# A Strassen form of the first channel product in a fused attention and MLP-mixer kernel

## Chip, cores and metric

The kernel runs on one core of one Trainium2 chip. The metric is the time of one execution on the device, in microseconds (us). A core has five engines that work side by side, each through its own queue in order: TensorE (PE; its weight loads are listed as PEld), VectorE (DVE), ScalarE (ACT), GpSimd (POOL) and SyncE (SP). TensorE writes its sums into eight banks of PSUM; the other engines empty them into SBUF.

## What is computed

Eight batches with eight heads of 576 rows and 64 columns; linear attention with random features (FAVOR), then a mixer of tokens and channels.

```python
q_s, k_s = q * scale, k * scale                  # scale = 64 ** -0.25
def phi(x):                                      # omega: 128 x 64
    h = x @ omega.T - sum(x * x) / 2
    return exp(h - max(h)) / sqrt(128)
kv, z = phi(k_s).T @ v, sum(phi(k_s), rows)
x = (phi(q_s) @ kv) / (phi(q_s) @ z + 1e-6)      # heads side by side: 8 x 576 x 512
h = relu(x.T @ w_tok1) @ w_tok2                  # 576 -> 256 -> 576, over tokens
u = x + h.T
out = u + relu(u @ w_ch1) @ w_ch2                # 512 -> 1536 -> 512, over channels
```

## The kernel before

The work is cut into *jobs*: one or a few instructions of one engine, with the jobs that they depend on and the places (PSUM banks, slots of rings of SBUF tiles) that they take and give back. The code makes all jobs in a fixed sequence, batch by batch, and numbers them as it goes. `ORDER` (L22) is a list, worked out beforehand, of these numbers: the order in which jobs are issued, and so the order of every engine's queue. Numbers below zero are warming matmuls. `SLOT` holds the place that each job takes; `MOVED` (L93) names the engine of a job where it is not the usual one. Nothing is planned while the kernel runs: each engine goes through its queue and waits on semaphores.

For each batch: `attention` (L521) projects keys and queries of four pairs of heads (L656, L668), takes exponentials on ScalarE (L514), the maximum over features on VectorE (L680) with a reciprocal (L682), scales v on GpSimd (`vs`, L689), multiplies keys with values (L701) and queries with that (L734, L736), and divides: `num_out` (L739) takes a reciprocal (L743) and a product (L744) on VectorE for each head, which gives `x`. `token_mix` (L764) makes the token products (L777, relu, L790), the sum `u` on VectorE (L793), and a DMA transposes `u` into `uT` (L798). Its first product needs all columns of `x` of its batch.

`channel_mix` (L955) works on 512 rows of a batch; the last 64 rows of all eight batches make a ninth chunk, the tail (`uTt`). Its first product is 12 blocks of 128 channels, each of four matmuls of 512 columns:

```python
for db in range(ND):
    nc.tensor.matmul(ps, wc1[:, db, cb * P : (cb + 1) * P], moving(db), start=(db == 0), stop=(db == ND - 1))
```

Each block takes a bank, and a relu (ScalarE, or VectorE by MOVED) writes it to `r3`. From batch 1 on the second product is done by `channel_out_fast` (L857) in a Strassen form (Winograd's): four sums `S` of quarters of `r3` on VectorE in two halves (L868 to L879), the sums `T` of weights made once (L448), seven products of 256 columns (L916), and seven `read`s on VectorE (L899) that add banks and `u` into the output tile `o`. Stores go out on SyncE's or ScalarE's queue, two of the tail on GpSimd's. Work of one batch's channel products, the next one's token products and the one after that's attention is interleaved in ORDER.

Of the kernel before, what the change touches and what calls it, by code (L numbers as in the profile page):

```python
# [9 lines left out]
FP32 = mybir.dt.float32  # L10
# [158 lines left out]
def kernel(  # L169
# [687 lines left out]
    def channel_out_fast(c, key, jr):  # L857
# [38 lines left out]
        def bank_of(b, j0):  # L896
            return (b, c, j0) if tail else (b, c)
# [173 lines left out]
```

## Time and profile before

| | |
|---|---|
| three runs | 276.75, 277.55, 277.63 us; median 277.55 |
| profiled execution | span 275.9 us, from the first to the last instruction; what lies around it is in the runs' times |
| busy share of the span | TensorE 97%, VectorE 81%, ScalarE 50%, GpSimd 33% |
| granted TensorE clock, mean | 0.996 |
| first product of the channels (L966) | 376 matmuls listed of batches 0 to 7, mean 379 ns each |
| second product (L916) | streams of 128x256 matmuls, mean 273 ns each |
| VectorE's largest groups | maximum L680 38.6 us, products L744 30.5, relus L292 27.7, reads L905 35.6 |
| start of the token products of batches 3 to 7 | 104.3, 133.5, 162.5, 189.5, 219.0 us |

A matmul's listed duration runs from its issue to the end of its passage through the array, and matmuls overlap; what one adds to a stream is the distance between two starts, which the chain of waits gives as time of a piece divided by its matmuls. Instructions of VectorE that are listed one behind the other can overlap a little in the same way.

### The profile page before, as it was taken

The numbers are of one execution on the slowest core, as the hardware profiler recorded it, in microseconds if no ns is written. First come the engines' busy times: TensorE is split into PE (matmuls) and PEld (weight loads), VectorE is DVE, ScalarE is ACT, GpSimd is POOL, SyncE is SP. The second block draws the span as 40 slices with busy tenths as digits, with TensorE's granted clock in tenths as the row PEclk, the third lists the DMA queues.
The fourth block names the chain that finished last, engine by engine and source line by source line (L and its number), as shares of the span: only waits on it lengthen the run. The fifth ranks groups of instructions, "written<-read, shape, count | busy, mean of one in ns | idle before, by whom it ended". The sixth has DMA issues, their size and how long they took to land.

```text
span 275.9 us, 6228 instructions
## 1 busy us (share of the span) xinstructions
PE 266.6 (97%) x2503; PEld 165.5 (60%) x2503; DVE 222.9 (81%) x462; ACT 138.1 (50%) x289; POOL 91.2 (33%) x115
## 2 busy tenths in 40 slices
PE   8789999999999999999999999999999999999993
PEld 3367455444567655755676656755676477446782
DVE  3897889876998799987999899978985992675992
ACT  3999941188685338734756456636654500040200
POOL 8994492063703490075019510600043000000001
PEclk9999999999999999999999999999999999999998
DMA  7999999999998999979989994840252304021125
GB/s 195 192 209 212 190 212 177 202 193 146 203 191 133 229 176 186 151 148 171 198 184 183 232 125 123 191 90 2 97 79 77 96 0 95 2 99 53 78 83 146
DMA packets 81292, 39.66 MB, mean 144 GB/s; under 512 B 63984, under 2 KB 77040, under 8 KB 81072
## 3 DMA queue, kind: packets, MB, share of 16 engines
q0 software_dynamic: 31744, 17.74, 44.2%
q1 hardware_dynamic: 47072, 15.50, 28.7%
q10 hardware_dynamic: 2448, 6.03, 5.6%
q8 instruction: 19, 0.31, 0.5%
q14 instruction: 9, 0.07, 0.1%
HBM read 35.95 MB, written 16.52 MB: 190 GB/s over the span
## 4 chain that ended last, share of the span: by engine, by line
PE 89%; DMA 6%; POOL 3%; DVE 0%; issue 0%; POOLq 0%
PE bank L966 33%; PE bank L916 25%; PE bank L777 5%; PE bank L790 5%; DMA w1m<-in_moe_w_tok_dram 4%; PE bank L1000 4%; PE bank L734 3%; PE bank L656 3%; PE bank L668 2%; PE bank L701 2%; DMA uT<-u 2%; POOL r L319 1%; PE bank L844 1%; PE bank L816 1%; PE bank L828 1%; PE bank L736 1%
## 5 line engine op out<-in xcount | busy, mean ns | idle before, releaser
L966 PE MATMUL bank<-uT,wc 128*128 128x512 f16 x376 | 90.4, 379 | 0.3 <-DMA uT<-u 0.3
L290 ACT ACTIVATE r<-bank 128x512 f16<-128x512 f32 (+1 forms) x84 | 46.9, 597 | 77.1 <-PE bank L966 62.0
L295 POOL TENSOR_TENSOR vs<-v,vs 128x512 f16<-128x512 f16 x31 | 33.2, 1074 | 91.2 <-DVE vs L682 60.5
L966 PEld LDWEIGHTS <-wc 128*128 128x128 f16 x424 | 38.3, 98 | 37.9 <-issue 1.1
L916 PEld LDWEIGHTS <-r 128*128 128x128 f16 x384 | 36.9, 98 | 8.1 <-issue 1.2
L514 ACT ACTIVATE kp<-bank 128x512 f16<-128x512 f32 x64 | 35.6, 622 | 10.4 <-PE bank L656 10.4
L514 ACT ACTIVATE qp<-bank 128x512 f16<-128x512 f32 x64 | 36.3, 616 | 8.9 <-PE bank L668 6.0
L680 DVE TENSOR_REDUCE km<-kp 128x8 f16<-128x1024 f16 x32 | 38.6, 1206 | 2.5 <-ACT kp L514 2.4
L292 DVE TENSOR_SCALAR r<-bank 128x512 f16<-128x512 f32 (+1 forms) x42 | 27.7, 672 | 12.0 <-PE bank L966 11.2
L744 DVE TENSOR_TENSOR x<-bank,rc 128x320 f16<-128x320 f32 x62 | 30.5, 492 | 2.1
L916 PEld LDWEIGHTS <-S 128*128 128x128 f16 x288 | 27.9, 98 | 5.4 <-issue 0.3
L905 DVE TENSOR_TENSOR o<-u,bank 128x512 f32<-128x512 f16 x28 | 19.0, 679 | 6.9 <-PE bank L916 6.8
L916 PE MATMUL bank<-T,r 128*128 128x256 f16 x192 | 23.8, 273 | 0.0
L916 PE MATMUL bank<-T,S 128*128 128x256 f16 x192 | 23.6, 273 | 0.0
L916 PE MATMUL bank<-wc,r 128*128 128x256 f16 x192 | 23.6, 273 | 0.0
L945 POOL DMA_DIRECT2D out_dram<-o x2 | 1.3, 648 | 60.9 <-issue 60.9
L793 DVE TENSOR_TENSOR u<-x,bank 128x512 f16<-128x512 f16 x28 | 17.8, 681 | 1.1 <-PE bank L790 1.0
L905 DVE TENSOR_TENSOR o<-o,bank 128x512 f32<-128x512 f32 (+1 forms) x27 | 16.6, 618 | 2.2 <-PE bank L916 1.6
L734 PEld LDWEIGHTS <-qp 128*128 128x128 f16 x256 | 13.8, 98 | 7.0 <-DVE kvsb L286 0.2
L734 PE MATMUL bank<-kvsb,qp 128*128 128x65 f16 x256 | 15.6, 193 | 0.0
L743 DVE RECIPROCAL rc<-bank 128x5 f32<-128x5 f32 x62 | 11.5, 186 | 4.1 <-PE bank L736 2.7
L701 PEld LDWEIGHTS <-kp 128*128 128x128 f16 x256 | 11.5, 98 | 5.1
(120 smaller groups left out, 376.3 us busy)
## 6 DMA issues: line engine op xcount, KB each, us to landing
out_dram<-o ACTq DMA_DIRECT2D x9, 512.0 KB, 2.6
q<-in_q_dram POOLq DMA_DIRECT2D x6, 576.0 KB, 7.2
wc<-in_moe_w_ch_dram POOLq DMA_DIRECT2D x4, 768.0 KB, 10.6
k<-in_k_dram POOLq DMA_DIRECT2D x6, 512.0 KB, 6.9
v<-in_v_dram POOLq DMA_DIRECT2D x6, 512.0 KB, 8.9
out_dram<-o SPq DMA_DIRECT2D x5, 512.0 KB, 3.9
r<-in_q_dram POOLq DMA_DIRECT2D x4, 288.0 KB, 7.3
v<-in_v_dram POOLq DMA_DIRECT2D x4, 256.0 KB, 8.7
```

The source lines that it names most:

```text
L290: nc.scalar.activation(out=out, in_=in_, func=AF.Relu)
L292: nc.vector.tensor_relu(out=out, in_=in_)
L295: (nc.gpsimd if eng == "POOL" else nc.vector).tensor_tensor(**kw)
L514: nc.scalar.activation(out=out, in_=in_, func=AF.Exp, bias=0.0, scale=1.0)
L680: nc.vector.reduce_max(out=mx, in_=kpv, axis=AX.X)
L701: nc.tensor.matmul(ps[:, i, :], kpv[:, 2 * i + j // 2, j % 2, :], vs[:, i * NJ + j, 0 : D + 1], start=(i == 0 and j == 0), stop=False, ski ...
L734: nc.tensor.matmul(ps[:, k, j * 65 : (j + 1) * 65], st, s[:, i, 0 : D + 1], start=True, stop=True)
L744: nc.vector.tensor_tensor(out=t_x[place("x", b)][:, :, (2 * hp + hs[0]) * D : (2 * hp + hs[0] + n) * D].rearrange("p j (i d) -> p i j d", ...
L793: nc.vector.tensor_tensor(out=t_u[place("u", b)][:, j, :], in0=t_x[place("x", b)][:, j, :], in1=bank(n), op=ALU.add)
L905: nc.vector.tensor_tensor(out=o, in0=a, in1=ps, op=ALU.add)
L916: nc.tensor.matmul(ps[:, j * DH : (j + 1) * DH], a[:, cb, j * P : (j + 1) * P], w[:, cb, :], start=(bank_of(b, j0) not in held and j == j0 ...
L966: nc.tensor.matmul(ps, wc1[:, db, cb * P : (cb + 1) * P], moving(db), start=(db == 0), stop=(db == ND - 1))
```

## The change

For batches 3 to 7 and the tail chunk (`FAST_IN = 3`) the first channel product is done by the new function `channel_in_fast`, in the same Strassen form. `u` and the weights are cut into quarters; four sums of quarters of `uT` (128x512 each) are made for each chunk (`usum` below), eight sums of weights (128x768 each) once, by `weight_sums`. The 1536 channels go in three thirds `m`. In each third there are seven products of four matmuls of 256 columns, in three banks: X takes P1, P6, P7 and P4 one after another, Y takes P2, Z takes P5 and P3. Between the products in X, ScalarE copies the bank to SBUF in fp32 (`keep`, three for each third). VectorE adds a kept product and a bank into `r3` (`join`, three for each third). Then come three relus: one from bank X (128x512), one over two quarters that stand in `r3` already (128x1024), one over the quarter from the third join (128x512).

The lists ORDER, SLOT and MOVED are new. For TensorE the new ORDER has the old sequence up to the last attention products of batch 3; from there on all engines have another order. MOVED now gives to GpSimd 16 of the 64 sums S, 11 of the 24 sums of `uT` and 3 of the 8 sums of weights, and gives to ScalarE 16 scalings `x = num * rc` (five activations each), of which batch 0 had two before. In ORDER the sums of GpSimd and VectorE's sums with two SBUF operands stand in turns.

Smaller edits: what were one job of a maximum with its reciprocal, or of a reciprocal with its product, are now two or three jobs with the same instructions (`km`, `kt_max`, `num_out`), with rings for their small tiles; the first and second halves' sums S depend on the sums that they read and no longer on the one before; the tail's output uses slots of `x` in place of `o`; the ring of `r1` has two places in place of three; five of the tail's stores change between SyncE's and ScalarE's queue. `SPLIT` and `HALVES` are empty, so what hangs on them is not issued.

```diff
+    FAST_IN = 3
+    SPLIT = ()
+    HALVES = ()
...
+    t_sum = sb([P, 2, DC // 2], FP16, "sum")
...
+            def km_rec(hp=hp):
                 with nc.allow_low_precision(reason="fp16 operand of the matmul"):
-                    nc.vector.reciprocal(out=vs[:, :, D], in_=mx)
-            j_m = add("DVE", 1.4, at_["km"], km, deps=je, take=[("vs", (b, hp))])
+                    nc.vector.reciprocal(out=t_vs[place("vs", (b, hp))][:, :, D], in_=t_km[place("km", (b, hp))])
...
+                    if e_num == "ACT":
                         for j in range(NJ + 1):
+                            nc.scalar.activation(out=to[:, j], in_=ps[:, j], func=AF.Copy, scale=rc[:, j : j + 1])
+                    else:
+                        nc.vector.tensor_tensor(out=to, in0=ps, in1=rc.unsqueeze(2).broadcast_to((P, NJ + 1, D)), op=ALU.mult)
...
-                job = add(e_sum, 0.5, key + KEYS["S"] + 0.1 * g + 0.01 * k, go, deps=[*need, *prev], take=[("S", c)])
-                prev = [job]
+                job = add(e_sum, 0.5, key + KEYS["S"] + 0.1 * g + 0.01 * k, go, deps=[*need, *([done[2 if k == 3 else 0]] if k else [])], take=[("S", c)])
+                done.append(job)
...
+    def weight_sums(key):
+
+        def quad(i, k, a):
+            return wc1[:, 2 * k + a, i * (DC // 2) : (i + 1) * (DC // 2)]
+        steps = (((1, 0), (1, 1), ALU.add), (0, (0, 0), ALU.subtract), ((0, 0), (1, 0), ALU.subtract), ((0, 1), 1, ALU.subtract))
+        for a in range(2):
+            done = []
+            for i, (x, y, op) in enumerate(steps):
+                e_sum = engine("DVE")
...
+    def channel_in_fast(c, key, jt):
+        def block(k, j):
+            return (t_uT[place("uT", c)] if c < B else uTt)[:, 2 * j : 2 * j + 2, 2 * k : 2 * k + 2, :].rearrange("p j a t -> p a j t")
+        def sums():
+            return t_uT[place("uT", ("sums", c))].rearrange("p i (a j) t -> p i a j t", a=2)
+        steps = ((lambda: block(0, 1), lambda: block(0, 0)), (lambda: block(1, 1), lambda: sums()[:, 0]), (lambda: block(1, 1), lambda: block(0, 1)),
+                 (lambda: block(1, 0), lambda: sums()[:, 1]))
...
+        ops = {
+            "P1": ("X", weights(0, 0), lambda: block(0, 0), []),
+            "P2": ("Y", weights(0, 1), lambda: block(1, 0), []),
+            "P5": ("Z", sum_weights(0), lambda: sums()[:, 0], [j_sums[0][0], j_sums[1][0], j_s[0]]),
+            "P6": ("X", sum_weights(1), lambda: sums()[:, 1], [j_sums[0][1], j_sums[1][1], j_s[1]]),
+            "P7": ("X", sum_weights(2), lambda: sums()[:, 2], [j_sums[0][2], j_sums[1][2], j_s[2]]),
+            "P4": ("X", weights(1, 1), lambda: sums()[:, 3], [j_s[3]]),
+            "P3": ("Z", sum_weights(3), lambda: block(1, 1), [j_sums[0][3], j_sums[1][3]]),
+        }
...
+        for m in range(NH // 2):
...
+                    for n in range(2):
+                        for a in range(2):
+                            nc.tensor.matmul(ps[:, n, :], w(a)[:, (2 * m + n) * P : (2 * m + n + 1) * P], x_[:, a],
+                                             start=(what in ("P1", "P2", "P5") and n == 0 and a == 0), stop=False, skip_group_check=True)
...
+            def keep(what, b, dep, m=m):
+                e_keep = engine("ACT")
+                def go(what=what, b=b, e_keep=e_keep, m=m, c=c):
+                    copy(e_keep, kept(what, m), bank(bank_of(b, m)))
+                return add(e_keep, 0.5, kk, go, deps=[dep], take=[part(what)])
...
+            def join(what, b, i, j, deps, free, m=m):
+                def go(what=what, b=b, i=i, j=j, m=m, c=c):
+                    nc.vector.tensor_tensor(out=r3(i, j, m), in0=kept(what, m).rearrange("p (n t) -> p n t", n=2), in1=pair(b, m), op=ALU.add)
...
+            p1 = product("P1", [])
+            p2 = product("P2", [])
+            p5 = product("P5", [])
+            k1 = keep("P1", "X", p1)
+            c11 = join("P1", "Y", 0, 0, [k1, p2], True)
+            p6 = product("P6", [k1])
+            k2 = keep("U2", "X", p6)
+            p7 = product("P7", [k2])
+            k3 = keep("U3", "X", p7)
+            c22 = join("U3", "Z", 1, 1, [k3, p5, c11], False)
+            p3 = product("P3", [c22])
+            c12 = join("U2", "Z", 0, 1, [k2, p3], True)
+            p4 = product("P4", [k3])
+            e_relu = engine("ACT")
+            def relu21(e_relu=e_relu, m=m, c=c):
+                relu_to(e_relu, r3(1, 0, m), pair("X", m))
...
+            def relu1(e_relu=e_relu, m=m, c=c):
+                t = t_r3[place("r3", c)][:, 2 * m : 2 * m + 2, :]
+                relu_to(e_relu, t, t)
...
+            def relu22(e_relu=e_relu, m=m, c=c):
+                relu_to(e_relu, r3(1, 1, m), r3(1, 1, m))
...
+        if c >= FAST_IN:
+            channel_out_fast(c, key, channel_in_fast(c, key, jt))
+            return
```

More of the change, by code (lines that the diff above doesn't have):

```diff
@@ new lines @@
+    909: "ACT", 963: "POOL", 964: "POOL", 965: "POOL", 966: "POOL", 982: "ACT", 996: "DVE", 1013: "ACT",
+    1016: "POOL", 1018: "POOL", 1019: "POOL", 1020: "POOL", 1021: "POOL", 1022: "POOL", 1037: "ACT", 1107: "ACT",
+    1141: "POOL", 1142: "POOL", 1157: "ACT", 1158: "ACT", 1172: "DVE", 1173: "ACT", 1189: "ACT", 1190: "ACT",
+    1195: "POOL", 1196: "POOL", 1197: "POOL", 1213: "ACT", 1214: "ACT", 1243: "DVE", 1249: "ACT", 1266: "ACT",
+    1277: "DVE", 1283: "ACT", 1297: "ACT", 1305: "DVE", 1336: "ACT", 1368: "ACT", 1391: "ACT", 1392: "ACT",
@@ L104 @@
+    1397: "POOL", 1415: "ACT", 1431: "ACT", 1448: "ACT",
 }
@@ L598, in kt_max @@
                 )
-            j_ktm = add("DVE", 1.2, kkt + 0.01, kt_max, deps=[*j_kte, j_msk], take=[("vbd", b)] if dma_in else [])
+            j_ktm = add("DVE", 0.15, kkt + 0.01, kt_mask, deps=[j_ktm, j_msk], take=take_vbd, give=[("kmt", b)])
             def vbd():
@@ L762, in attention @@
+                last_x.append(add(e_num, 0.45, kno, scale, deps=[j_r], take=[("x", b)], give=[at, ("rc", (b, hp, hs[0]))]))
         return last_x
@@ L865, in channel_out_fast @@
             part = slice(g * NH // 2, (g + 1) * NH // 2)
-            need = [jr[cb + NH * e] for cb in range(part.start, part.stop) for e in range(2)]
+            need = [x for cb in range(part.start, part.stop) for e in range(2) for x in jr[cb + NH * e]]
             steps = (
@@ L897, in bank_of, with o_tag, o_of, go @@
             return (b, c, j0) if tail else (b, c)
+        def o_tag(i):
+            return ("x", ("o", i)) if tail else ("o", (c, i))
+        def o_of(i):
+            if tail:
+                return t_x[place(*o_tag(i))].rearrange("p j d -> p (j d)")[:, 0 : 4 * DM].bitcast(FP32).rearrange("p (j d) -> p j d", j=2)
+            return t_o[place(*o_tag(i))]
         def read(k, b, i, e, base, deps, free, j0=0, j1=2):
-            def go(c=c):
-                o = t_o[place("o", (c, i))][:, j0:j1, DH * e : DH * e + DH]
+            e_read = engine("DVE")
+            def go(c=c, e_read=e_read):
+                o = o_of(i)[:, j0:j1, DH * e : DH * e + DH]
                 ps = bank(bank_of(b, j0)).rearrange("p (j d) -> p j d", j=2)[:, j0:j1]
+                if e_read == "ACT":
+                    nc.scalar.copy(out=o, in_=ps)
+                    return
                 u = t_u[place("u", c)] if c < B else t_ut
@@ L944, in store @@
                         to = out[4 * i : 4 * i + 4, SM:S, cols].rearrange("(j h) t d -> h t j d", h=2)[h]
-                        (nc.scalar if eng == "ACT" else nc.sync if eng == "SP" else nc.gpsimd).dma_start(out=to[:, js], in_=t_o[place("o", (c, i))][half[h], js, cols])
-                    dma(eng, key + 0.9, 0.3, store, deps=[outs[need, j] for j in range(*js)], give=[("o", (c, i))],
+                        (nc.scalar if eng == "ACT" else nc.sync if eng == "SP" else nc.gpsimd).dma_start(out=to[:, js], in_=o_of(i)[half[h], js, cols])
+                    dma(eng, key + 0.9, 0.3, store, deps=[outs[need, j] for j in range(*js)], give=[o_tag(i)],
                         cost=0.412 if js[1] - js[0] == 1 else 0.414)
@@ L951, in store @@
             def store(i=i, eng=eng):
-                (nc.scalar if eng == "ACT" else nc.sync).dma_start(out=out[c, 0:SM, :].rearrange("(p j) d -> p j d", j=NJ)[:, 2 * i : 2 * i + 2, :], in_=t_o[place("o", (c, i))])
-            dma(eng, key + 0.9 + 0.1 * i, 1.3, store, deps=[outs[x, 0] for x in need], give=[("o", (c, i))], cost=0.4)
+                (nc.scalar if eng == "ACT" else nc.sync).dma_start(out=out[c, 0:SM, :].rearrange("(p j) d -> p j d", j=NJ)[:, 2 * i : 2 * i + 2, :], in_=o_of(i))
@@ new lines, in channel_out_fast, with sum_of, go @@
+            dma(eng, key + 0.9 + 0.1 * i, 1.3, store, deps=[outs[x, 0] for x in need], give=[o_tag(i)], cost=0.4)
+    j_sums = []
+    def sum_of(i, k):
+        n = 2 * i + k
+        if n < 6:
+            tag = "qT" if n < 3 else "kT"
+            return (t_qT if n < 3 else t_kT)[place(tag, "sums")][:, n % 3 * (DC // 2) : n % 3 * (DC // 2) + DC // 2]
+        return t_sum[:, n - 6]
+    def weight_sums(key):
[3 more added lines that the diff above has]
+        for a in range(2):
+            done = []
+            for i, (x, y, op) in enumerate(steps):
+                e_sum = engine("DVE")
+                def go(i=i, a=a, x=x, y=y, op=op, e_sum=e_sum):
+                    x, y = [sum_of(z, a) if isinstance(z, int) else quad(*z, a) for z in (x, y)]
+                    tt(e_sum, out=sum_of(i, a), in0=x, in1=y, op=op)
+                need = [done[z] for z in (x, y) if isinstance(z, int)]
+                n = 2 * i + a
+                done.append(add(e_sum, 0.46, key, go, deps=[*need, *j_wc1], take=[("qT" if n < 3 else "kT", "sums")] if n < 6 else []))
+            j_sums.append(done)
@@ L984, in relu @@
                 relu_to(e_relu, t_r3[place("r3", c)][:, cb, :], bank(n))
-            jr[cb] = (add(e_relu, 0.5, key + 0.5 * pos / NCB, relu, deps=[j1], take=[("r3", c)], give=[("bank", n)]))
+            jr[cb] = [add(e_relu, 0.5, key + 0.5 * pos / NCB, relu, deps=[j1], take=[("r3", c)], give=[("bank", n)])]
         if fast:
@@ L1001, in channel_mix @@
                 prev = add("PE", mm(4, 512) + (mm(4, P) if part == 2 else 0.0), key + 0.5 + 0.5 * (3 * j + part) / 12, c2,
-                           deps=[prev, *jr[4 * part : 4 * part + 4], *j_wc2], take=[("bank", n)], give=[("r3", c), ("uT", c)])
+                           deps=[prev, *(x for done in jr[4 * part : 4 * part + 4] for x in done), *j_wc2], take=[("bank", n)], give=[("r3", c), ("uT", c)])
             k2 = key + 0.5 + 0.5 * (3 * j + 3) / 12
```

175 lines of the change are left out of this document (119 added, 56 removed), and 132 rows, old and new, of the table ORDER.

## The prediction

> **What bounds the kernel now.** I read the shares of busy time first, then the chain that ended last, then the waits of TensorE, then busy time stage by stage.
>
> ```profile
> PE 266.6 (97%) x2503; PEld 165.5 (60%) x2503; DVE 222.9 (81%) x462; ACT 138.1 (50%) x289; POOL 91.2 (33%) x115
> ...
> PE 89%; DMA 6%; POOL 3%; DVE 0%; issue 0%; POOLq 0%
> ```
>
> TensorE (PE) carries nine tenths of the chain, VectorE (DVE) none of it. The change sits in the last three fifths, so I cut that part where TensorE starts the first token product (L777) of batches 3 to 7; the last cut, at 247.9, lies in the last products.
>
> ```profile
> 104.30 1.83 PE bank L777 x8
> ...
> 234.09 13.81 PE bank L966 x64
> ...
> 260.94 10.51 PE bank L916 x96
> ...
> 271.48 0.42 DVE o L905
> ...
> 104.30:133.50 29.20, 29.20 (x290) 18.64 (x290) 25.71 (x55) 16.09 (x33) 9.58 (x11) 1.00 1.03 162
> 133.50:162.50 29.00, 29.00 (x279) 18.30 (x279) 26.52 (x57) 17.48 (x37) 12.19 (x14) 1.00 1.10 198
> ...
> 247.90:276.00 28.10, 23.54 (x193) 18.54 (x190) 18.96 (x39) 2.43 (x5) 1.29 (x2) 0.96 0.28 94
> sum 171.70, PE 167.14 PEld 108.48 DVE 138.57 ACT 72.06 POOL 33.13; mean PE 27.86 PEld 18.08 DVE 23.10 ACT 12.01 POOL 5.52
> ```
>
> The columns of a stage are its length, then busy us of PE, weight loads (PEld), DVE, ACT, POOL, the granted clock, DMA. TensorE is busy in every us until 271.5, at a granted clock of 1.00, and no wait of TensorE is listed after 104.3. So this part lasts as long as its matmuls, and DVE, at 91% in the second stage shown, has just enough time. The last DVE instruction ends at 271.9, and the stores take the 4.0 us to the end of the span.
>
> **What it takes off TensorE.** Before, one chunk's first channel product is 48 matmuls of 512 columns; the row at 234.09 gives 13.81/64 = 0.216 us for each, 10.36 us in all. After, it is 7 products x 3 thirds x 4 = 84 matmuls of 256 columns. The row at 260.94 is such a stream (the second product is already done this way): 10.51/96 = 0.109 us each, 9.20 us. That is 1.16 us a chunk, and over batches 3 to 7 and the tail chunk **7.0 us**. All of it is on the path, so if nothing else came late the span would be 275.9 - 7.0 = 268.9 us.
>
> **What it puts on the other engines.** These rows price it:
>
> ```profile
> L905 DVE TENSOR_TENSOR o<-o,bank 128x512 f32<-128x512 f32 x21 | 14.1, 674 | 1.6 <-PE bank L916 1.1 <-issue 0.2
> L292 DVE TENSOR_SCALAR r<-bank 128x512 f16<-128x512 f32 x40 | 26.9, 684 | 11.7 <-PE bank L966 11.2
> L295 DVE TENSOR_TENSOR S<-S,r 128x768 f16<-128x768 f16 x16 | 8.7, 552 | 0.0
> L448 DVE TENSOR_TENSOR T<-wc 128x1536 f16<-128x1536 f16 x2 | 1.9, 950 | 0.0
> L744 DVE TENSOR_TENSOR x<-bank,rc 128x320 f16<-128x320 f32 x62 | 30.5, 492 | 2.1
> L290 ACT ACTIVATE r<-bank 128x512 f16<-128x512 f32 x82 | 46.1, 602 | 76.6 <-PE bank L966 62.0 <-PE bank L777 8.9 <-DVE o L905 5.4
> L290 ACT ACTIVATE r<-bank 128x256 f16<-128x256 f32 x2 | 0.8, 384 | 0.4 <-PE bank L817 0.4
> L756 ACT ACTIVATE x<-bank,rc 128x64 f16<-128x64 f32 x10 | 2.3, 340 | 0.0
> L295 POOL TENSOR_TENSOR vs<-v,vs 128x512 f16<-128x512 f16 x31 | 33.2, 1074 | 91.2 <-DVE vs L682 60.5 <-PE bank L668 22.3 <-PE bank L966 4.5
> L295 POOL TENSOR_TENSOR T<-vt,T 128x1024 f16<-128x1024 f16 x1 | 1.9, 1941 | 0.0
> ```
>
> I number the jobs in the order in which the code makes them, before and after, and read the engine of each from MOVED; the numbers of jobs so counted are exactly those in ORDER.
>
> VectorE gains 54 joins (9 a chunk; a kept product in SBUF plus a bank, as in the L905 row): 54 x 0.674 = 36.4 us. It gains 13 sums of u (128x512 in SBUF; the L295 and L448 rows give 0.52 ns an element, so 0.42 us): 5.5. Also 5 sums of weights at 0.552: 2.8; 4 relus of a bank at 0.684 and one more token relu: 3.4. Then 9 relus over 1024 and 6 over 512 elements, from SBUF to SBUF in fp16, of which no row shows the like: at the rate of the SBUF sums above 0.69 and 0.42 us, and half of that as the low end (one operand less to read); 4.4 to 8.7 us, and I take 6.3, as no row decides between the ends. It loses 28 relus of the old product at 0.684 (19.2), 16 sums S that go to GpSimd at 0.552 (8.8), 14 scalings that go to ScalarE at 0.492 (6.9), and 2 small copies (0.6). Net **+18.9 us** (17 to 21.3): from 104.3 on, VectorE has 138.6 + 18.9 = **157.5 us** of work.
>
> ScalarE (ACT) gains 54 keeps, 14 relus of a bank and 12 of SBUF at 0.602 (48.2), 9 relus of 1024 elements (602 and 384 ns for 512 and 256 make 1.04 us; 9.4), 14 scalings of five activations each (2.3 us for ten, so 16.1), less 44 old relus (26.5) and small change: 72.1 + 47 = 119 us of some 168, 71%. GpSimd gains 19 sums of 768 elements (1.5 us, between its two rows) and 11 of 512 (1.07): 33.1 + 40 = 73 us, 44%. Neither is a bound. The split of the small DVE steps into jobs adds no instruction.
>
> **The new waits.** In each third the products P1, P6, P7 and P4 go one after another through bank X, and TensorE's P6, P7 and P4 wait until ScalarE has kept what stands there. TensorE takes its queue in order, so whatever ORDER has behind such a product waits too. One third's chain is 4 x (0.44 + 0.60) = 4.2 us against 9.2 us of products in a chunk, with three thirds and the attention of the next batch interleaved: ORDER has other work to put between, and I cost this at nothing. If that cover were gone, each missed keep would cost up to 0.6 us. P3 waits for the join of bank Z on VectorE, whose queue is the full one. Stores and loads keep their queues; the tail's output moves to an x tile, which takes a possible wait for o away and gains nothing on TensorE's path, since there is none.
>
> **What is late next.** Without any stall TensorE would let VectorE's last read end at 271.9 - 7.0 = 264.9, so 160.6 us for 157.5 us of work: 98%. How full has VectorE been while TensorE did not wait?
>
> ```profile
> 100.00:120.00 20.00, 20.00 (x182) 12.63 (x180) 19.37 (x38) 13.62 (x27) 5.40 (x8) 1.00 1.07 164
> 160.00:180.00 20.00, 20.00 (x187) 13.11 (x186) 19.15 (x35) 11.96 (x24) 5.29 (x6) 1.00 0.77 146
> ```
>
> 97% and 96%, over 20 us each. I take 96% over the whole part: 157.5/0.96 = 164.1, so the span is 104.3 + 164.1 + 4.0 = **272.4 us**, which is 3.5 us of stalls out of the 7.0 gained. Counting VectorE's and TensorE's work in the new ORDER between the first token products of batches 3, 4, 5, 6 and 7 puts the stalls in place. Instructions that stand close overlap at their ends, so I count 0.60 us for a 0.68 us one, as three in a row show, and take the kinds that the change leaves alone (the largest are the two below it) at their own rows:
>
> ```profile
> 109.60 1.88 DVE L793 TENSOR_TENSOR u<-x,bank 128x512 f16<-128x512 f16 x3
> ...
> L680 DVE TENSOR_REDUCE km<-kp 128x8 f16<-128x1024 f16 x32 | 38.6, 1206 | 2.5 <-ACT kp L514 2.4
> L743 DVE RECIPROCAL rc<-bank 128x5 f32<-128x5 f32 x62 | 11.5, 186 | 4.1 <-PE bank L736 2.7 <-ACT r L290 0.8
> ```
>
> Each stage, VectorE against TensorE: 31.3 to 29.7, 29.1 to 26.9, 23.1 to 23.6, 29.4 to 29.4; then less on VectorE until the last products. The first two stages have 3.8 us too much for VectorE; since every token product waits for VectorE's scalings of its batch, that excess must surface there unless the two queues stand several us apart.
>
> The runs shown have a median of 277.55 us against the span of 275.9, so 1.65 us lie around the span: 272.4 + 1.65 = **274.0 us**.
>
> **Rivals.**
>
> *TensorE stays the bound.* If the short relus cost their low end, VectorE has 155.6 us of work, and a well packed order hides nearly all: 268.9 + 1.65 = 270.5 us, up to 272. For it: ScalarE and GpSimd have room, and the window from 100 shows 97%. Against it: the excess of the first two stages. 0.20.
>
> *VectorE becomes the bound at the density it has now.* In the fullest stage above it reaches 26.52/29.0 = 91%. At that share 157.5/0.915 = 172.1 us, the span is 280.4 and the time 282: slower. It decides below 94%, where 157.5/0.94 + 104.3 + 4.0 + 1.65 is 277.5. For it: joins need a product of TensorE and a keep of ScalarE, so VectorE waits at times it cannot make good. Against it: at 91% nothing pressed VectorE, since TensorE was the bound. 0.19.
>
> *GpSimd's sums stop VectorE's.* The trace shows two such meetings.
>
> ```profile
> 14.52 1.02 DVE L295 TENSOR_TENSOR vs<-v,vs 128x512 f16<-128x512 f16 x1
> 14.96 1.50 POOL L295 TENSOR_TENSOR vs<-v,vs 128x512 f16<-128x512 f16 x1
> ...
> 118.46 1.06 POOL L295 TENSOR_TENSOR vs<-v,vs 128x512 f16<-128x512 f16 x1 [0.34 <-DVE vs L682]
> 119.10 0.46 DVE L593 TENSOR_TENSOR vbd<-rct,mask 128x8 f16<-128x8 f16 x1
> ...
> 140.32 0.19 DVE L593 TENSOR_TENSOR vbd<-rct,mask 128x8 f16<-128x8 f16 x1
> ```
>
> A GpSimd sum that starts inside VectorE's takes 1.50 instead of 1.07, and a tiny VectorE product that starts inside GpSimd's takes 0.46 instead of 0.19, ending with it: one holds the other off. [...] The change has 30 more GpSimd sums. If 10 of them met one of VectorE's sums and each cost VectorE half a sum, 0.75 us, 7.5 us would come on top of 274.0: 281.5. From five such meetings (3.7 us) the gain is gone. ORDER speaks against it: the two kinds stand in turns, with stretches of some 20 us of TensorE's work that have only GpSimd's or only VectorE's. But ORDER fixes the order on each engine only, and the engines may drift apart. 0.10.
>
> *Weight loads are no longer hidden.* The change has 84 loads a chunk for 48. A load of 98 ns laid bare each time would cost 36 x 0.098 - 1.16 = 2.4 us a chunk, 14 us in all: 291 us.
>
> ```profile
> L916 PEld LDWEIGHTS <-r 128*128 128x128 f16 x384 | 36.9, 98 | 8.1 <-issue 1.2
> ```
>
> This row and the stream of 0.109 us a matmul at 260.94, each with its own load, exclude it. [...] 0.01.
>
> **Numbers.** Three runs spread over 0.3%, which is about what can be told from no change; that band is 276.7 to 278.4, met by VectorE shares of 93.5 to 94.5%, and gets 0.08. The forecast, shares of 94.5 to 97%, 272 to 276.7, gets 0.42; with the first rival, faster has 0.62. Slower has 0.19 + 0.10 + 0.01 = 0.30. The range starts at 270.3, just under TensorE's own bound, and reaches to 281, into both slower rivals, leaving out about 0.15.
>
> **What would show it.** In the profile after: L966 loses 288 matmuls and 504 of 256 columns appear, about 0.109 us each without a wait; VectorE's busy time rises from 222.9 to about 242 us, 90% of the span; TensorE shows, for the first time after 104, waits of 2 to 6 us in all, for VectorE's scalings, joins or sums, most of them around the token products of batches 4 to 6; ScalarE near 185 us. It is wrong if TensorE's gaps are long and stand at keeps of ScalarE, if VectorE's SBUF sums take visibly over 0.55 us, or if VectorE has idle time while TensorE waits.

## The result and the profile after

The changed kernel takes 280.7 us (median of 20 runs), the kernel before beside it on the same chip 277.2 us (20 runs): a ratio of 1.0099, 95% interval 1.0078 to 1.012, so it is slower by 1%. Some runs of the changed kernels below are several us longer than the others of the same kernel; a ratio compares undisturbed runs, a median takes all. The forecast was 274.0 us, faster; 280.7 lies in its range (270.3 to 281.0), on the wrong side of no change. That it lies inside is luck: the range reached so far for two rivals in which VectorE is late, and these are not what the runs below show.

The page of the changed kernel, its busy times and its chain:

```profile
PE 264.1 (95%) x2719; PEld 188.3 (68%) x2719; DVE 234.5 (84%) x494; ACT 180.1 (65%) x405; POOL 133.8 (48%) x145
...
PE 64%; DMA 16%; DVE 6%; ACT 5%; issue 3%; POOL 3%; SPq 0%; DVEq 0%; POOLq 0%; ACTq 0%
```

TensorE carried 89% of the chain and DMA 6%; now DMA carries 16%, with `kT<-k` and `uT<-u` at its head (7% and 5% of the span). TensorE's waits say the same:

```profile
PE bank L1076 <- DMA uT<-u: 2.9, 2, 1.5
PE bank L682 <- DMA kT<-k: 2.3, 1, 2.3
...
PE bank L799 <- DVE x L789: 0.5, 1, 0.5
```

L1076 is the Strassen product, L682 the projection kp, L799 the tail of t1 (the first token product); the columns are the sum, the number and the longest. TensorE waits 1.5 us for uT of batch 3, 2.3 us for kT of batch 6 and 1.4 us for uT of batch 7. After 104 us no wait of 0.5 us or more names VectorE.

The matmuls themselves do what was forecast. Two pieces that follow each other without a gap in TensorE's timeline (start, length):

```profile
234.69 2.34 PE L1076 MATMUL bank<-uT,wc 128*128 128x256 f16 x20 [1.39 <-DMA uT<-u]
236.88 1.47 PE L964 MATMUL bank<-T,r 128*128 128x256 f16 x12
```

2.19 us for 20 matmuls are 0.110 us each. So where is the gain lost? The first token products of batches 3 to 7 are marks that both kernels have (L777 before, at 104.23, 133.40, 162.40, 189.44 and 218.88 us in the timeline). After, those of batches 3 and 5 (the others are at 136.36, 192.31 and 221.14 us):

```profile
105.57 1.90 PE L806 MATMUL bank<-x,w1m 128*128 128x512 f16 x8
...
167.41 1.90 PE L806 MATMUL bank<-x,w1m 128*128 128x512 f16 x8
```

The distances of these marks, for the two kernels and for versions that come below (us):

| kernel | to batch 3 | 3 to 4 | 4 to 5 | 5 to 6 | 6 to 7 | 7 to end | span |
|---|---|---|---|---|---|---|---|
| before | 104.2 | 29.2 | 29.0 | 27.0 | 29.4 | 57.0 | 275.9 |
| after | 105.6 | 30.8 | 31.1 | 24.9 | 28.8 | 57.3 | 278.4 |
| after, without later loads | 104.8 | 30.6 | 27.1 | 24.9 | 28.8 | 57.4 | 273.6 |
| after, six sums back, rc in turn, kt later | 103.4 | 32.4 | 27.1 | 24.8 | 28.8 | 57.5 | 273.9 |
| after, all three causes away | 104.2 | 30.8 | 27.1 | 24.8 | 28.8 | 55.5 | 271.1 |
| before, two of them away | 103.8 | 29.1 | 29.0 | 27.0 | 29.4 | 57.2 | 275.6 |

At the first token product of batch 5 the changed kernel is 5.0 us late; from there it is 2.5 us quicker than the kernel before. The new order moves some work over these marks, so a column shows a place, and only the whole row is a balance.

What is late before batch 5? GpSimd's queue first, around the loads of k6, v5 and q6, before and then after:

```profile
123.46 0.56 POOL L364 DMA_DIRECT2D k<-in_k_dram  x1
...
126.76 0.92 POOL L337 DMA_DIRECT2D v<-in_v_dram  x1
127.67 0.54 POOL L359 DMA_DIRECT2D q<-in_q_dram  x1
```

```profile
120.07 1.15 POOL L318 TENSOR_TENSOR uT<-uT 128x512 f16<-128x512 f16 x1 [5.08 <-DMA uT<-u]
...
126.65 0.59 POOL L387 DMA_DIRECT2D k<-in_k_dram  x1
127.25 1.65 POOL L318 TENSOR_TENSOR S<-r,S 128x768 f16<-128x768 f16 x1
128.84 1.71 POOL L393 DMA_DIRECT2D k<-in_k_dram  x2
130.56 1.65 POOL L318 TENSOR_TENSOR sum<-wc,qT 128x768 f16<-128x768 f16 x1
132.15 0.94 POOL L360 DMA_DIRECT2D v<-in_v_dram  x1
133.09 0.53 POOL L382 DMA_DIRECT2D q<-in_q_dram  x1
```

A sum of uT waits 5.08 us for its transposing DMA at the head of the queue, and sums S and of weights stand between the loads: k6 goes out 3.2 us later, v5 and q6 5.4 us. kT of batch 6 is asked for at the same time in both (136.7 and 137.0 us), and is now on its way beside v5 and q6 (issued at 132.2 and 133.1 us, 9.3 and 11.6 us to landing) and beside two stores of o (9.0 and 9.1 us) instead of one (4.2). The DMA issues between 80 and 245 us, before and then after (count, median us from issue to landing):

```profile
uT<-u SPq DMA_TRANSPOSE x6, 5.1
qT<-q SPq DMA_TRANSPOSE x4, 6.1
kT<-k SPq DMA_TRANSPOSE x4, 5.6
```

```profile
uT<-u SPq DMA_TRANSPOSE x6, 5.7
qT<-q SPq DMA_TRANSPOSE x4, 6.9
kT<-k SPq DMA_TRANSPOSE x4, 8.9
```

The median of kT went from 5.6 to 8.9 us; kT of batch 6 landed in 10.7 us instead of 6.1. That the loads issued by GpSimd slow the transposes issued by SyncE is a guess from these rows; the runs without the later loads test it.

### The profile page after: what moved, and what is told of

Read it like the earlier page. It is cut to its first block, busy times and chain, and to the rows that moved or that the text cites. A ratio compares the mean times of both kernels' runs of the same rounds, so it can differ in the third digit from the quotient of the medians.

```text
span 278.4 us, 6902 instructions
## 1 busy us (share of the span) xinstructions
PE 264.1 (95%) x2719; PEld 188.3 (68%) x2719; DVE 234.5 (84%) x494; ACT 180.1 (65%) x405; POOL 133.8 (48%) x145
## 4 chain that ended last, share of the span: by engine, by line
PE 64%; DMA 16%; DVE 6%; ACT 5%; issue 3%; POOL 3%; SPq 0%; DVEq 0%; POOLq 0%; ACTq 0%
PE bank L1076 18%; PE bank L964 18%; DMA kT<-k 7%; PE bank L1147 6%; DMA uT<-u 5%; PE bank L806 4%; PE bank L682 2%; DMA k<-in_k_dram 2%; PE bank L1181 2%; PE bank L819 2%; PE bank L771 2%; PE bank L738 2%; PE bank L694 2%; ACT kp L537 2%; DMA wc<-in_k_dram 2%
## 5 line engine op out<-in xcount | busy, mean ns | idle before, releaser
L313 ACT ACTIVATE r<-bank 128x512 f16<-128x512 f32 (+1 forms) x53 | 30.5, 594 | 21.8 <-PE bank L806 9.1
L1147 PE MATMUL bank<-uT,wc 128*128 128x512 f16 x136 | 32.9, 379 | 0.0
L1076 PE MATMUL bank<-uT,wc 128*128 128x256 f16 x192 | 26.2, 273 | 2.9 <-DMA uT<-u 2.9
L1076 PEld LDWEIGHTS <-wc 128*128 128x128 f16 x216 | 20.6, 98 | 5.6 <-DMA uT<-u 1.6
L789 DVE TENSOR_TENSOR x<-bank,rc 128x320 f16<-128x320 f32 x48 | 23.1, 486 | 1.1
L944 DVE TENSOR_TENSOR o<-u,bank 128x512 f32<-128x512 f16 x28 | 18.9, 677 | 4.2 <-PE bank L964 2.9
L309 ACT COPY r<-bank 128x512 f32<-128x512 f32 x18 | 10.0, 613 | 17.6 <-PE bank L1076 17.5
L999 POOL DMA_DIRECT2D out_dram<-x x2 | 1.3, 641 | 40.4 <-DVE x L944 40.4
L1147 PEld LDWEIGHTS <-wc 128*128 128x128 f16 x136 | 12.1, 98 | 12.2 <-issue 1.1
L787 ACT ACTIVATE x<-bank,rc 128x64 f16<-128x64 f32 x80 | 18.2, 340 | 1.7 <-DVE rc L778 1.6
L1076 PE MATMUL bank<-uT,qT 128*128 128x256 f16 x108 | 18.9, 273 | 0.0
L1076 PE MATMUL bank<-uT,kT 128*128 128x256 f16 x108 | 18.5, 272 | 0.1
```

What stands on the lines that cost most here:

```text
L313: nc.scalar.activation(out=out, in_=in_, func=AF.Relu)
L787: nc.scalar.activation(out=to[:, j], in_=ps[:, j], func=AF.Copy, scale=rc[:, j : j + 1])
L789: nc.vector.tensor_tensor(out=to, in0=ps, in1=rc.unsqueeze(2).broadcast_to((P, NJ + 1, D)), op=ALU.mult)
L944: nc.vector.tensor_tensor(out=o, in0=a, in1=ps, op=ALU.add)
L1076: nc.tensor.matmul(ps[:, n, :], w(a)[:, (2 * m + n) * P : (2 * m + n + 1) * P], x_[:, a], start=(what in ("P1", "P2", "P5") and n == 0 and ...
```

## The experiments

**Theory A**: TensorE waits for DMA transposes, since GpSimd's new sums delay its loads and the shorter products cover less of the way of kT and uT. **Theory B**: VectorE is the limit. Each ratio is against the kernel before on the same chip.

**Loads ahead of the sums** in GpSimd's queue:

```diff
+EARLIER = [([863, 862], 601), ([1040, 868, 1039], 482)]
```

The first pair puts k5 ahead of the first of these weight sums, the second k6's tails, v5 and q6 ahead of a sum S of batch 2.

> The changed kernel, but on GpSimd's queue the loads that came behind its new sums go first: the casts of batch 5's keys ahead of the two sums of weights, and batch 6's key tails, v and query cast ahead of the last sum S of batch 2 and the third sum of weights. Nothing else moves. Theory A (late loads collide with the DMA transposes that TensorE waits for): the keys of batch 6 land in 6 to 7 us after issue in place of 10.7, u of batch 3 in about 6 in place of 8.3; TensorE's waits of 2.3 and 1.5 us and the 3.4 us at half clock go; 3 to 6 us faster than the changed kernel, 274 to 277 us, ratio to before 0.99 to 1.00. Theory B (VectorE too full, TensorE waits only show it at a DMA): the waits move elsewhere, ratio stays at 1.01.

Measured: 279.96 us, 1.0083 (1.0057 to 1.011). The wait at kT of batch 6 is gone, but kT of batch 4 is now waited for 1.8 us, and the weight sum that stands behind the loads 1.2 us. uT of batch 3 took 7.9 us, not about 6. One wait was traded for others.

**Six sums back on VectorE** (in `MOVED`; three sums of weights, 601, 602, 604, and three sums S of batch 2, 476, 477, 482; two expectations below call all six weight sums, which is wrong; here the six entries stand in one line):

```diff
-    476: "POOL", 477: "POOL", 482: "POOL", 601: "POOL", 602: "POOL", 604: "POOL",
```

> The changed kernel, but the six sums of GpSimd that stand ahead of those loads (three of weights, three S of batch 2) go back to VectorE; the order of the jobs is the same. VectorE gets 6 x 0.55 = 3.3 us more. Theory A: the loads are early, as in the kernel with the loads first, and that outweighs VectorE's 3.3 us: ratio to before 0.99 to 1.00. Theory B: VectorE is the scarce engine, so 1 to 3 us slower than the changed kernel, ratio 1.015 to 1.02.

Measured: 278.35 us, 1.0042 (1.0023 to 1.0062). More work on VectorE (236.6 us) makes it faster, against theory B.

**The kernel before with late loads** (`spare_sums` stands ahead of batch 5's cast of keys and of its load of v):

```diff
+    def spare_sums(n):
+        for _ in range(n):
+            nc.gpsimd.tensor_tensor(out=t_ktt[0], in0=wc1[:, 0, 0 : H * RT], in1=wc1[:, 1, 0 : H * RT], op=ALU.add)
...
+            spare_sums(8 if b == 5 else 0)
```

> The kernel before, with GpSimd held up where the change holds it up: eight spare sums of 256 elements (about 0.65 us each, 5 us together) on GpSimd ahead of the cast of batch 5's keys and eight ahead of batch 5's load of v, behind which stands batch 6's query cast. No product is saved and VectorE does what it did. Theory A: transposes of keys, queries or u land in 8 to 11 us in place of 5 to 6 and TensorE waits 1 to 4 us for them: ratio to before 1.005 to 1.015. Theory B: nothing waits for GpSimd here, ratio 1.000 within 0.003.

Measured: 288.44 us, 1.0423 (1.0404 to 1.0441), far more than expected. The kernel that had no such wait after 104 us now waits 3.4 us for uT, 2.2 for qT and 1.4 for kT, and its mean clock falls from 0.996 to 0.979, which over 287.6 us of span is some 5 of the 11 us. The spare sums took 6.5 and 5.9 us, not 5, and qT of batch 6 landed after 25.2 us instead of 6.3.

**Without 15 relus on VectorE** (leaves out the SBUF relus of the Strassen product that are VectorE's; the second of its two places is not shown):

```diff
-                relu_to(e_relu, t, t)
+                if e_relu == "ACT":
+                    relu_to(e_relu, t, t)
```

> The changed kernel without the 15 relus from SBUF to SBUF on VectorE (9 of 1024 and 6 of 512 elements; 5.4 us of VectorE's time), so r3 keeps negative values there. Theory A: VectorE is not what TensorE waits for, time within 1 us of the changed kernel, ratio 1.007 to 1.012. Theory B: 3 to 5 us faster than the changed kernel, ratio 0.992 to 1.00.

Measured: 279.42 us, 1.0079 (1.0052 to 1.0105), an interval that overlaps the changed kernel's. Its waits:

```profile
PE bank L1076 <- DMA uT<-u: 2.9, 3, 1.4
PE bank L682 <- DMA kT<-k: 2.8, 1, 2.8
```

VectorE's busy time is 3.7 us lower and TensorE waits for the same transfers. Theory B falls as the main cause.

**Without the later loads**, on both kernels (the first two lines stand in each load of k, q and v; the changed kernel still loads v once):

```diff
+            if b >= 4:
+                return
...
-                nc.sync.dma_start_transpose(out=t.unsqueeze(1), in_=scratch[w, b])
+                nc.sync.dma_start_transpose(out=t.unsqueeze(1), in_=scratch[w, min(b, 3)])
```

> The changed kernel, but from batch 4 on the fp16 copies of q and k aren't made and v isn't loaded (but once): the DMA transposes of q and k of batches 4 to 7 stay and read the copy of batch 3. Theory A (GpSimd's load transfers, issued late, stretch the DMA transposes, and TensorE waits for these): the transposes of kT and uT from 100 us on land in 4 to 6 us as in the kernel before, the waits of 2.3 us at kp and about 1.5 of the 2.9 us at the first channel product go, and the half-clock spell with them; 1.5 to 5 us faster than the changed kernel, so 275.5 to 278.5 us, ratio to the kernel before 0.995 to 1.005. Theory C (the new order simply asks for kT and uT too early; the loads are beside the point): the landings may shorten, the waits at kT of batch 4 and uT of batches 3 and 7 stay, under 1 us faster, ratio 1.007 to 1.011.

> Control: the kernel before with the same left out (no fp16 copies of q and k and no loads of v from batch 4 on; the transposes read the copy of batch 3). All theories: no wait of TensorE stood at a DMA in that part before, so nothing is to be gained: ratio 0.997 to 1.002; the transposes land up to 1 us sooner.

Measured: the changed kernel 275.46 us, 0.9948 (0.9929 to 0.9966); the kernel before 278.05 us, 1.0043 (1.0025 to 1.0061). The loads alone cost the changed kernel 1.5%, some 4 us, and the kernel before nothing; why the control is 0.4% slower stays open. The same view of landings:

```profile
uT<-u SPq DMA_TRANSPOSE x6, 5.0
qT<-q SPq DMA_TRANSPOSE x4, 5.3
kT<-k SPq DMA_TRANSPOSE x4, 5.4
```

kT is back at its time of before, the column from batch 4 to 5 falls from 31.1 to 27.1, and 2.7 us of waits at uT remain, where about half was expected to go. The 1.5% hold the half clock that followed the wait at kT (last section), which is gone too (mean clock 1.000, after 0.994).

**The places of rc in turn.** In the new list SLOT the place of a reciprocal (L778) is used again by the next one, which must wait until the product x (L789) has read it. VectorE's timeline after, then with the places in turn:

```profile
70.72 0.19 DVE L778 RECIPROCAL rc<-bank 128x5 f32<-128x5 f32 x1
70.95 0.49 DVE L789 TENSOR_TENSOR x<-bank,rc 128x320 f16<-128x320 f32 x1
71.55 0.20 DVE L778 RECIPROCAL rc<-bank 128x5 f32<-128x5 f32 x1
```

```profile
70.36 0.18 DVE L782 RECIPROCAL rc<-bank 128x5 f32<-128x5 f32 x1
70.58 0.49 DVE L793 TENSOR_TENSOR x<-bank,rc 128x320 f16<-128x320 f32 x1
70.99 0.18 DVE L782 RECIPROCAL rc<-bank 128x5 f32<-128x5 f32 x1
```

```diff
+                    if tag == "rc":
+                        i = turn % self.places[tag]
+                        turn += 1
```

> The changed kernel, with the eight places of the reciprocal rc taken in turn instead of by the list SLOT. Theory A (a reused place makes each next reciprocal wait for the product before it): reciprocals of a batch follow each other after 0.62 us instead of 0.85, the wait of about 1 us at t1's tail of batch 2 around 75 us shrinks or goes, 0.5 to 1.5 us faster than the changed kernel, ratio to the kernel before 1.003 to 1.008. Theory B (VectorE as a whole limits the last part): VectorE saves some 0.2 us for each of 62 pairs, 5 us or more faster, ratio 0.98 to 0.995. Rival: the place doesn't matter: 1.009 to 1.012.

Measured: 280.24 us, 1.012 (1.0101 to 1.014), a miss. The pairs follow each other after 0.63 us instead of 0.83, TensorE's wait at the tail of t1 in batch 2 is gone and batch 3's mark stands at 103.3 us instead of 105.6; but the wait at kT of batch 6 grows from 2.3 to 3.3 us. What comes earlier only waits longer for the same transfer.

**Three edits together**: six sums back, rc in turn, and on TensorE kt and the first kp of batch 4 later and two products of `out` ahead of the Strassen products of batches 3 and 7.

```diff
+EARLIER = [([693, 703, 694, 704, 695], 757), ([491, 495], 613), ([1207, 1211], 1353)]
```

> Three edits to the changed kernel together: six weight sums back on VectorE, so that GpSimd issues the loads sooner; the places of rc in turn; and on TensorE kt and the first kp of batch 4 after the last third of t1, two of out's products of batch 2 ahead of the first product of batch 3, and two of out's of batch 6 ahead of the first of batch 7, so that each reads its transposed tile later. Theory A (TensorE's waits for transposes took what the matmuls saved): waits at kT and uT together fall from 5 to under 2 us, ratio 0.985 to 0.995, so 273 to 275.5 us. Theory B (VectorE is the limit): six sums more on VectorE make it no faster than the version with these sums alone, 1.004, but for the reciprocals. If what it waits for only moves: 1.000 to 1.004.

> The changed kernel with the six weight sums back on VectorE and the places of rc in turn, without the three moves on TensorE. Theory A: the 1.0042 of the weight sums alone less 0.5 to 1.0 us for the wait at t1's tail of batch 2, so 1.000 to 1.003 (277 to 278 us); the waits at the two channel products of batches 3 and 7 stay at about 2.5 us together. If a wait taken away early only lets the next transposes be asked for earlier against the same loads: 1.004 to 1.008.

> The version with the six sums (three weight sums and three of batch 2's sums S) back on VectorE and the places of rc in turn, and of the three moves on TensorE the first alone: kt and the first kp of batch 4 after the token products of batch 3. Theory A: the version without the move had 0.9923; the wait of 0.7 us at kT of batch 4 goes as well, 0.988 to 0.993. The run with all three moves had 1.0084, so one of them costs over 4 us: if it is this one (kp and what stands behind it late), 1.004 to 1.010; if it is the two moves of out's products (which wait for the reads into o and its stores), 0.988 to 0.995.

Measured: all three moves 280.9 us, 1.0084 (1.0048 to 1.012); none of them 276.0 us, 0.9923 (0.9898 to 0.9949); the first alone 276.37 us, 0.9967 (0.9938 to 0.9995). So the moves of `out` were wrong. With them TensorE waits for the reads into o, which themselves wait 3.2 us for stores of o:

```profile
PE bank L978 <- DVE o L958: 3.4, 3, 2.1
```

The two versions without them are faster than the kernel before, by 0.3 to 0.8%; their intervals just overlap, so whether the move of kt matters is not settled. Sums and places together gain more than the two runs alone (1.0042 and 1.012) let expect.

**Only the later half of the change**: before's order and product up to the token products of batch 5, then the changed kernel.

```diff
-    FAST_IN = 3
+    FAST_IN = 5
```

ORDER, SLOT and MOVED (not shown) are those of the two kernels, joined there.

> Only the later half of the change: up to the token products of batch 5 the order, the engines and the places are those of the kernel before, with the old first channel product for batches 3 and 4 (the eight weight sums go to GpSimd behind the load of q of batch 6, where its queue is empty); from there on it is the changed kernel, with the Strassen product for batches 5 to 7 and the tail chunk. In the profiles the first token product of batch 5 starts at 162.4 us before and at 167.4 us after, and from there to the end are 113.5 and 111.0 us. Theory A (the loss lies where the loads and the DMA transposes share the rings, up to about 160 us, and the matmuls saved behind that are kept): 162.4 + 111.0 = 273.4 us of span, 274 to 276 us, ratio to the kernel before 0.988 to 0.995. Theory B (VectorE has too much work wherever the Strassen product stands): the stage of batch 5 loses what the earlier ones lost, 1.000 to 1.006. If the gain behind 167.4 us was only work that the new order had pulled ahead of it: 0.998 to 1.002.

> The run with only the later half of the change again, with the eight weight sums in other places: three on GpSimd behind the load of q of batch 6 (while VectorE divides by the denominators of batch 4), three on GpSimd behind the last product for vs of batch 5, two on VectorE ahead of the sums S of batch 4. In the first such run eight of them in a row on GpSimd held VectorE's sums S of batch 3 at 1.9 us each instead of 0.55, TensorE waited 4.8 us behind them and its clock was halved after that. Theory A (only the weight sums were in the way; the matmuls saved from batch 5 on are kept): VectorE's sums S are 0.55 us again, 274 to 276.5 us, ratio to the kernel before 0.990 to 0.998. Theory B (the later half gains nothing by itself): 0.999 to 1.006.

Measured: 285.4 us, 1.0284 (1.0257 to 1.031), then 277.3 us, 1.0013 (0.9988 to 1.0039). In the first, sums of VectorE and GpSimd hold each other up. VectorE, then GpSimd, at the same time:

```profile
134.51 1.99 DVE L224 TENSOR_TENSOR S<-S,r 128x768 f16<-128x768 f16 x1
136.42 1.99 DVE L224 TENSOR_TENSOR S<-r 128x768 f16<-128x768 f16 x1
```

```profile
134.13 1.95 POOL L224 TENSOR_TENSOR qT<-wc 128x768 f16<-128x768 f16 x1
136.16 1.83 POOL L224 TENSOR_TENSOR kT<-qT,wc 128x768 f16<-128x768 f16 x1
```

VectorE's 0.55 us become 1.99; its two sums end at 136.50 and 138.41 us, 0.4 us after GpSimd's (136.08 and 137.99). The second run keeps them apart and still gains nothing, as the second theory of its expectation had it. In its profile batch 5's mark stands at 164.5 us, not 162.4, after a wait of 1.3 us for a relu of VectorE. From there it takes 113.4 us, not 111.0: it waits 2.1 us for uT of batch 7, and 1.7 us go to the half clock behind that wait (0.83 on average from 230 to 240 us). The profiled run took 279.8 us, the median is 277.3, so that part can be shorter; whether the 111.0 us of the changed kernel hold work that its order had done ahead of the mark is not shown. (That loads and transposes "share the rings", as the first expectation has it, is not shown. Between 80 and 245 us q0 moves 6.97 MB after and 0.79 without the later loads, q1 11.01 in both; before, from 228.2 to 232 us, where a transpose is the only transfer issued, all packets are in q1: the page lists the loads in q0 and the transposes in q1.)

**Is that all?** The transposes of u from batch 3 on read the u of the batch before, so they need not wait for the sums that make u ("early u" below); then this with rc in turn and without the later loads; and a control:

```diff
-                in_=t_u[place("u", b)].rearrange("p j d -> p (j d)"),
+                in_=t_u[place("u", b - 1 if b >= 3 else b)].rearrange("p j d -> p (j d)"),
```

> The changed kernel, but the DMA transposes of u of batches 3 to 7 read the u of the batch before, so they need not wait for the sums that make u (the data are those of another batch; the number and size of the transfers stay). Theory A (the way from u through the transposing DMA to the first channel product is as long as before, while the matmuls that covered it are shorter): the waits of 1.5 and 1.4 us at uT of batches 3 and 7 go, 2 to 3 us faster than the changed kernel, ratio to the kernel before 0.999 to 1.004; the waits at kT stay. Rival (only the loads matter): 1.007 to 1.011.

> The changed kernel with all three supposed causes taken away together: no fp16 copies of q and k and no loads of v from batch 4 on (but one load of v), the transposes of u from batch 3 on read the u of the batch before, and the places of rc in turn. Theory A (these three are what took the 7.0 us that the matmuls save): 275.5 us without the loads, less 2.7 us of waits at uT, less 1.0 us at t1's tail of batch 2: 271.0 to 273.0 us, ratio to the kernel before 0.978 to 0.985. If something else takes a good part of the gain, VectorE for one: 0.988 to 0.995.

> Control: the kernel before with the first two of these (no copies and loads from batch 4 on, transposes of u that need not wait for u). TensorE had no wait there, so nothing is gained: ratio 0.998 to 1.005 (without the loads alone it was 1.0043).

Measured: 278.73 us, 0.9993 (0.9968 to 1.0019) for u alone; 272.36 us, 0.9825 (0.9808 to 0.9843) for all three; 277.46 us, 1.0008 (0.9992 to 1.0023) for the control. With the three causes away the change is worth 272.36 - 277.46 = -5.1 us, of the 7.0 that its matmuls save.

The first of these runs does not price uT alone. Its waits at uT are gone, but against the expectation the 2.3 us at kT of batch 6 are gone too: with the transposes of u issued at other times, kT landed in 6.2 us instead of 10.7. Without the loads, early u and rc in turn together bring 3.1 us (275.46 to 272.36).

Part of the rest shows in the waits with all three away, and VectorE's and GpSimd's timelines say what VectorE was late with:

```profile
PE bank L979 <- DVE o L959: 1.5, 1, 1.5
```

```profile
113.63 1.57 DVE L322 TENSOR_TENSOR kT<-wc 128x768 f16<-128x768 f16 x1
115.13 1.51 DVE L322 TENSOR_TENSOR r<-r 128x768 f16<-128x768 f16 x1
116.56 0.67 DVE L959 TENSOR_TENSOR o<-u,bank 128x512 f32<-128x512 f16 x1
```

```profile
113.61 1.16 POOL L322 TENSOR_TENSOR uT<-uT 128x512 f16<-128x512 f16 x1
114.86 1.36 POOL L322 TENSOR_TENSOR uT<-uT,uT 128x512 f16<-128x512 f16 x1
```

GpSimd's sums of uT no longer wait for their DMA and now meet two sums of VectorE, which take 1.57 and 1.51 us instead of 0.55. By these durations the read behind them comes 2.0 us later, more than the 1.5 us that TensorE waits. The run with early u alone has the same meeting (1.62 and 1.50 us).

**Why uT lands late** is not settled by these runs. After, the transposes of u of batches 3 and 7 (SyncE's timeline) are each followed by a store of 512 KB (ScalarE's timeline) about 1 us later, and the product waits:

```profile
111.67 1.88 SPq L827 DMA_TRANSPOSE uT<-u  x1
112.62 0.34 ACTq L1006 DMA_DIRECT2D out_dram<-o  x1
120.04 1.92 PE L1076 MATMUL bank<-uT,wc 128*128 128x256 f16 x16 [1.49 <-DMA uT<-u]
```

```profile
228.63 2.46 SPq L827 DMA_TRANSPOSE uT<-u  x1
229.71 0.34 ACTq L1006 DMA_DIRECT2D out_dram<-o  x1
```

| | uT of batch 3, issue to landing | until TensorE comes to it | uT of batch 7, issue to landing | until TensorE comes to it |
|---|---|---|---|---|
| before | 5.9 | 6.9 | 4.3 | 6.8 |
| after | 8.3 | 6.9 | 6.0 | 4.7 |
| after, without later loads | 8.1 | 6.9 | 6.0 | 4.7 |

So the cover became shorter for batch 7 only, both transfers became longer, and the loads are not the reason. With the landings of before neither would have been waited for. In the kernel before no store was issued while these two were on their way. No run moves the stores, so they are a likely cause, not a shown one.

## Why the prediction was wrong

**The saving** was sized rightly: 0.110 us a matmul against 0.109.

**"Stores and loads keep their queues"**, with no cost put beside it: this step failed. The order of the loads among themselves was kept, but the prediction itself counted 40 us more of sums on GpSimd and did not ask which DMAs are queued behind them. They delayed loads by up to 5.4 us, and the loads' absence is worth 1.5%. Nor did it ask which transfers the new order would send out beside each other, the stores among them.

**"So this part lasts as long as its matmuls"**: true of before, where no transfer came late, and carried over to after without a look at issue, landing and first use of each. This is the second failed step: the sum has no term for a transfer that TensorE waits for. After 104 us TensorE waits 2.9 us for uT and 2.5 for kT, and 1.7 us go to the half clock. With the 1.3 us that the mark of batch 3 is late, these are 8.4 us against the 7.0 saved, so 1.4 of the 2.5 us that the span grew; the rest stays open. That these waits cost the time is shown by the runs without the loads and with early u; why uT itself takes longer to land is not.

**"I cost this at nothing"**, said of the products that wait for ScalarE's keeps, held: no wait of TensorE at a keep is listed after 104 us.

**"The split of the small DVE steps into jobs adds no instruction"**: true and beside the point. Each new job takes a place, and the places, used again at once, put 0.2 us between pairs. TensorE reached the first token product of batch 2 at 76.8 us, before at 75.3, with the places in turn at 74.8: 1.5 to 2 us, before the part that I examined began. Taken away alone this gains nothing (1.012).

**VectorE as what is late next**: not shown by the runs as a main cause. It has 234.5 us busy, not 242; its SBUF relus cost 0.42 and 0.28 us:

```profile
L315 DVE TENSOR_SCALAR r<-r 128x1024 f16<-128x1024 f16 x9 | 3.7, 419 | 0.1
L315 DVE TENSOR_SCALAR r<-r 128x512 f16<-128x512 f16 x6 | 1.6, 280 | 0.0
L1100 DVE TENSOR_TENSOR r<-kp,bank 128x512 f16<-128x512 f32 x18 | 11.9, 675 | 0.7 <-PE bank L1076 0.6
```

5.4 us in all where I took 6.3; a join costs the 0.675 of its row. Most of the difference is a slip in the sum: it added whole durations to a busy time in which overlapped ends count once. The durations listed for VectorE add up to 260.2 us, before to 242.8, so 17.4 more against 18.9 forecast, but busy time grew by 11.6. Waits of 2 to 6 us came as announced, but at DMAs.

**The rivals.** None named the DMA queues. GpSimd's sums do not stop VectorE's in the changed kernel (sums S stay at 0.55 us). They do in the joined version, whose order does not keep them apart (1.99 us), and, once the engines drift as that rival feared, in the two runs with early u, where waits of TensorE of 1.8 us (u alone) and 1.5 us (all three) stand behind such a meeting. ScalarE (180.1 us against 185) and GpSimd (133.8 against 131) came out near.

## What to carry to other kernels

A stretch of matmuls is also a cover (that of uT of batch 7 went from 6.8 to 4.7 us): before shortening it, list what lands under it (issue, landing, first use) and take the slack away from each; look also at what other transfers the new order issues beside it. Work given to an engine that issues loads is paid for by whatever stands behind it in that queue, even where the engine is idle half the time (GpSimd, 48% busy here, sent loads out up to 5.4 us later). When one wait goes and the next grows by as much, take the suspected causes away together, and on the kernel before as well.

## What the runs showed of the hardware

After some of TensorE's waits its granted clock fell to 0.5. Behind the 2.3 us at kT of batch 6, in windows of 5 us (length, then PE, PEld, DVE, ACT, POOL, the granted clock, DMA share, GB/s):

```profile
145.00:150.00 5.00, 2.72 (x35) 1.95 (x33) 3.16 (x6) 2.20 (x7) 4.30 (x6) 0.89 1.24 211
150.00:155.00 5.00, 5.00 (x65) 4.36 (x63) 3.19 (x10) 2.91 (x13) 4.70 (x7) 0.77 1.19 149
```

The clock's record has 0.5 for 3.41 us there; I count half of that, some 1.7 us, as work lost on top of the wait. Behind the wait of 3.3 us with rc in turn it fell too (0.66 on average from 145 to 150 us), behind the one of 2.8 us without the relus it did not (1.00 in every window of 5 us from 140 to 160). What decides between the two is not shown.

Sums of VectorE and GpSimd that ran side by side took longer on both engines (first run with the later half): VectorE's 0.55 us became 1.99, and GpSimd's 1.65 became 1.83 to 1.95. Beside GpSimd's sums of 512 elements VectorE's took 1.5 to 1.6 us (early u, and all three causes away).
